# Softmax denominators inverted on one row per head and spread through device memory, normalisation by 512 columns, no clip, last products on the whole array

## The chip, the cores and the metric

The kernel runs on one NeuronCore of a Trainium2 chip. The metric is device time in microseconds of one execution (lower is better). The engines have these names in the profile: PE (matrix products), PEld (its weight loads), ACT (ScalarE), DVE (VectorE), POOL (GpSimd) and SP (SyncE, which here only issues transfers). Each takes its instructions strictly in the order in which the program lists them; an instruction that waits holds up all that are listed behind it on its engine. The order is fixed when the program is built.

## The reference

Two attention blocks read the same input, and a gate per token mixes them.

```python
def _A_ref(x, wq, wk, wv, wo):          # x: 1 x 2048 x 512, 32 heads of 16; one key and one value head
    q = (x @ wq).reshape(B, S, H, Dh).transpose(0, 2, 1, 3)
    k = x @ wk
    v = x @ wv
    p = _softmax(jnp.einsum("bhqd,bkd->bhqk", q, k) * (Dh ** -0.5), axis=-1)
    o = jnp.einsum("bhqk,bkd->bhqd", p, v)
    return o.transpose(0, 2, 1, 3).reshape(B, S, H * Dh) @ wo

def _B_ref(x, wqkv, wo):                # 32 heads with keys and values of their own
    ...

g = _sigmoid((x * gate_w).sum(-1, keepdims=True))
return g * a + (1 - g) * b              # a, b: the two blocks
```

All arrays are float32: x is 2048 by 512, the projections are 512 by 512 or narrower.

## The kernel before

**Groups and exps.** The 64 heads are worked in eight groups (`groups`: source "a" or "b", index 0 to 3) of eight heads. A group has two halves of 1024 queries; a half has four sums, numbered `s`, each for four pairs of a head and 512 queries over the 16 chunks `c` of 128 keys. A block is one head, one chunk and 512 queries. `scores(u)` makes two blocks with PE (keys on partitions, queries along the free dimension) in one of two PSUM tiles `sc`, and ACT takes their exp in one instruction of 128x1024 (line 569). There are 2048 such units, and some of them, listed in `vector`, don't go to ACT: `vector_scores` puts their products into a spare pair of PSUM banks, and DVE works out the exp by a polynomial in nine instructions: two of line 581, two of line 587 (`part`), five of line 592 (`horner`). `choose` decides while the program is built which units these are.

**Sums.** `values` multiplies the exps with the values and, in the same product, with ones, so that a sum has in each band of 32 rows 16 rows of the output and 16 equal rows of the denominator. Four banks `aux` form two pairs: one gathers the running sum, the other (`spare()`) is free for all other products, one at a time. After the last chunk `emptied` adds the two banks of the pair into `raw` with DVE (lines 229 and 230), and eight transfers from SP's queue take the denominators to a tile `dT` and the outputs to a tile `oT` (128 rows, 512 queries). When the second sum of a pair has come (`s % 2`), `norm_pieces` gives the side list eight tasks: four reciprocals of 128x128 (line 497), then four times a multiplication, a rounding to 16 bits and a remainder (lines 504 to 506). Each of the four adds one `o_unit`: three products of a 128-token tile with `wo` in 64x32 pieces of the PE array into two spare banks, then two additions to `acc` by DVE (line 485).

**Order.** `_Tasks` is a planner that runs while the program is built. It goes through the exps one after another (`EXP` = 916 ns each), keeps a clock for PE and a clock `busy` for DVE, and lists work when its numbers say that there is room: products from `units` (by due time), DVE tasks from `side` (each with an earliest step and a duration in ns; they are listed in the order of that step), polynomial pieces from `fill`. `late()` tells that products are behind and holds back new polynomial exps. `hurry` lists all side tasks that are due, before a sum is emptied. `flush` lists what is left after the last exp. The planner knows nothing of transfers: a side task of so many ns is reckoned to run at once.

**Other parts that the change touches.** `project` makes q and k from `x` (two additions, a clip by `QK_MAX`, line 394, then the split into two 16-bit parts). `flag_stats` collects the largest absolute values of inputs on DVE near the end (line 234); a flag from them selects a general path that isn't taken in these runs.

Below, a number of an exp counts ACT's instructions of line 569 (line 601 in the changed kernel) in the program's order from 0; a DVE or PE instruction "at exp 452" is one listed behind that exp and ahead of the next.

Of the kernel before, what the change touches and what calls it, by code (L numbers as in the profile page):

```python
# [12 lines left out]
F32 = mybir.dt.float32  # L13
# [7 lines left out]
P = 128  # L21
# [53 lines left out]
class _Tasks:  # L75
# [87 lines left out]
    def flush(self):  # L163

        assert not self.moves and not self.fill
        ahead = 0
        while self.open or self.units or self.side:
            if self.side and ahead < 6 and not (self.units and ahead > 2):
                self.side.popleft()[1]()
                ahead += 1  # L170
                continue
            ahead -= 3
# [15 lines left out]
def _fast(ctx, tc, x, wq_a, wk_a, wv_a, wo_a, wqkv_b, wo_b, gate_w, out, flag):  # L188
# [8 lines left out]
    ps_x = ctx.enter_context(tc.tile_pool(name="ps_x", bufs=1, space=PSUM))  # L197

# [127 lines left out]
    def kv_products(b, i, bank):  # L326
# [11 lines left out]
        k32 = ops.tile([P, 4, DH], F32, tag="k32", name=f"k32{b}")  # L338
# [25 lines left out]
    def project(w, needs, name, kind, n0, half, parts, put, queues, late=None):  # L364
# [16 lines left out]
        def product(i, c, a, b, first, last):  # L381
# [12 lines left out]
            nc.vector.tensor_scalar(y, y, QK_MAX, -QK_MAX, op0=ALU.min, op1=ALU.max)  # L394
# [72 lines left out]
    oT, dT, o16s = {}, {}, {}  # L467
# [23 lines left out]
    def norm_pieces(src, gi, half, t8, last):  # L491
        j, cols = t8 // 4, slice(t8 % 4 * P, (t8 % 4 + 1) * P)
        ends = last and half and j

        def over():
            d = dT[src, gi, half, j][:, cols]
            nc.vector.reciprocal(d, d)  # L497

        def parts():
            o, d = oT[src, gi, half, j][:, cols], dT[src, gi, half, j][:, cols]  # L500
            if t8 % 4 == 0:
                o16s[src, gi, half, j] = ops.tile([P, 2, BLK], F16, tag="o16", name=f"o16{src}{gi}{half}{j}", bufs=5)
            o16 = o16s[src, gi, half, j][:, :, cols]
            nc.vector.scalar_tensor_tensor(o, o, UP, d, op0=ALU.mult, op1=ALU.mult)
            (nc.scalar.copy if ends else nc.vector.tensor_copy)(o16[:, 0], o)  # L505
            (nc.gpsimd if ends else nc.vector).tensor_sub(o16[:, 1], o, o16[:, 0])
            todo.add([o_unit(src, gi, 8 * half + t8, o16, last)], todo.now + 4,
                     min(todo.now + 280, ends_by() - (0 if last and half else 60)))

        return [over, parts]  # L510
# [107 lines left out]
    def emptied(m):  # L618
        quad = blocks[4 * m : 4 * m + 4]
        n, half, s, c = quad[0][:4]  # L620
        src, gi = groups[n]
        todo.hurry()
        raw = ops.tile([P, BLK], F32, tag="raw", name=f"raw{src}{gi}{half}{s}", bufs=1)
        added(raw, aux[turn[0]], 1.0)
        j = quad[0][5]
        if s % 2 == 0:
            oT[src, gi, half, j] = ops.tile([P, BLK], F32, tag="oT", name=f"oT{src}{gi}{half}{j}", bufs=1)
            dT[src, gi, half, j] = ops.tile([P, BLK], F32, tag="dT", name=f"dT{src}{gi}{half}{j}", bufs=1)
        ends = m // NT == len(blocks) // 4 // NT - 1
        queues = (nc.sync, nc.scalar, nc.gpsimd) if ends else (nc.sync,)  # L630
        for a, part in enumerate((dT, oT)):
            for i, (_, _, _, _, p, _, hh) in enumerate(quad):
                rows = slice((2 * p + hh) * DH, (2 * p + hh + 1) * DH)

                at = 32 * i + (DH if (src == "a" or hh == 0) == (part is dT) else 0)
                queues[(4 * a + i) % len(queues)].dma_start(part[src, gi, half, j][rows], raw[at : at + DH, :])
        last = n == len(groups) - 1
        if s % 2:
            over, parts = zip(*[norm_pieces(src, gi, half, t8, last) for t8 in range(4 * j, 4 * j + 4)])
            todo.add_side(over, todo.now + (4 if last and half else 10), [950])  # L640
            todo.add_side(parts, todo.now + (4 if last and half else 13), [800])

    def flag_stats():
        absmax("v_a", 0, vA[:, :, :DH], AX.XY)
        for c in range(NK):
            absmax("x", c, xT[:, 0, c, :])
        absmax("gate", 0, wkv[:, :, 2 * DH])
        absmax("wk_a", 0, wkv[:, :, :DH], AX.XY)
        absmax("wv_a", 0, wkv[:, :, DH : 2 * DH], AX.XY)
# [23 lines left out]
    def begin(n, half):  # L673
# [291 lines left out]
```

## Time and profile before

| what | value |
|---|---|
| time, median of 3 runs | 1909.49 us (1907.66 to 1913.36) |
| the profiled execution: its own time | 1907.7 us |
| its span | 1905.9 us |
| mean granted PE clock | 0.992 |
| ACT busy | 1831.9 us |
| PE busy | 1800.7 us |
| DVE busy | 1382.3 us |
| first exp starts, last exp ends | 29.28 us, 1876.55 us |

The busy shares are of the whole span. PE's share counts pipelined matmuls whose ends are modelled, so 94% doesn't mean that PE has no room; the waits and the idle time ahead of an instruction tell which engine the others wait for.

### The profile page before, as it was taken

How to read it: one execution, taken by the hardware profiler on the slowest of the kernel's cores; microseconds unless marked ns; L12 is line 12 of the kernel's file. 1: busy time of each engine (PE TensorE's matmuls, PEld its weight loads, DVE VectorE, ACT ScalarE, POOL GpSimd, SP SyncE). 2: the span in 40 equal slices, each digit the busy share in tenths (PEclk: the TensorE clock that was granted, in tenths of full speed). 3: DMA queues.
4: the chain of work that ended last, by engine and by line, in shares of the span. 5: the costliest groups of instructions: out<-in, count | busy, mean ns of one | idle time of the engine just before them, and what ended most of it. 6: DMA issues, size and time to landing. Idle time of an engine off the chain costs nothing.

```text
span 1905.9 us, 128055 instructions
## 1 busy us (share of the span) xinstructions
PE 1800.7 (94%) x59664; PEld 1124.5 (59%) x59664; DVE 1382.3 (73%) x2095; ACT 1831.9 (96%) x1997; POOL 466.3 (24%) x840
## 2 busy tenths in 40 slices
PE   7999999999999999999999999999999999999985
PEld 4666665555566665665555656656655666665642
DVE  5367668787888765778788873788888867477762
ACT  4999999999999999999999999999999999999984
POOL 5333302330044230323006502042203433030000
PEclk9999999999999999999999999999999999999997
DMA  4121101110022110111002201020101111011101
GB/s 141 27 49 35 35 15 27 42 35 16 12 43 46 29 37 12 41 32 35 12 21 45 52 19 31 19 54 15 32 15 36 39 38 37 10 37 35 40 26 42
DMA packets 55739, 65.03 MB, mean 34 GB/s; under 512 B 21440, under 2 KB 29632, under 8 KB 55200
## 3 DMA queue, kind: packets, MB, share of 16 engines
q0 software_dynamic: 24112, 24.89, 6.8%
q1 hardware_dynamic: 30400, 31.46, 6.3%
q8 instruction: 469, 7.68, 1.7%
q14 instruction: 70, 0.57, 0.1%
q10 hardware_dynamic: 688, 0.43, 0.1%
HBM read 10.55 MB, written 4.19 MB: 8 GB/s over the span
## 4 chain that ended last, share of the span: by engine, by line
ACT 67%; PE 15%; issue 12%; DVE 4%; DMA 1%; SPq 0%; DVEq 0%; ACTq 0%; POOL 0%
ACT pr L569 67%; PE aux L613 7%; PE sc L562 4%; PE aux L225 4%; DVE stats L234 1%; DVE acc L485 0%; DVE vpr L592 0%; DMA acc<-in_A_x_dram 0%; DVE dTb L497 0%; DMA dTb<-rawb 0%; PE aux L300 0%; DVE v L238 0%; DVE yv L230 0%; DVE yv L229 0%; DVE xT L305 0%
## 5 line engine op out<-in xcount | busy, mean ns | idle before, releaser
L569 ACT ACTIVATE pr<-sc 128x1024 f32<-128x1024 f32 x1974 | 1821.3, 1090 | 24.7 <-PE sc L562 21.1
L613 PE MATMUL aux<-pr,vA 64*32 64x256 f32 x15712 | 647.2, 376 | 2.0 <-issue 1.8
L613 PE MATMUL aux<-pr,vB 64*32 64x256 f32 x15872 | 636.4, 376 | 0.6 <-issue 0.4
L562 PE MATMUL sc<-Qa,kA 64*32 64x512 f16 x7856 | 441.2, 380 | 28.0 <-ACT pr L569 4.7
L562 PE MATMUL sc<-Qb,K 64*32 64x512 f16 x7936 | 426.2, 381 | 31.0 <-ACT pr L569 5.6
L592 DVE SCALAR_TENSOR_TENSOR vpr<-vpr,part 128x1024 f32<-128x1024 f32 x296 | 363.5, 1228 | 6.1
L562 PEld LDWEIGHTS <-K 64*32 64x32 f16 x8192 | 203.3, 89 | 276.8 <-issue 195.3
L613 PEld LDWEIGHTS aux<-pr,vA 64*32 64x32 f32 x15712 | 328.6, 105 | 57.8 <-issue 9.8
L613 PEld LDWEIGHTS aux<-pr,vB 64*32 64x32 f32 x15872 | 316.6, 106 | 53.9 <-issue 4.6
L562 PEld LDWEIGHTS <-kA 64*32 64x32 f16 x8192 | 203.5, 89 | 238.8 <-issue 157.8
L485 DVE SCALAR_TENSOR_TENSOR acc<-aux,gate_up,acc 128x512 f32<-128x512 f32 x240 | 180.1, 750 | 126.6 <-PE aux L225 112.2
L375 POOL DMA_DIRECT2D Qb<-hib x128 | 63.0, 492 | 557.0 <-PE sc L562 553.9
L375 POOL DMA_DIRECT2D Qa<-hia x118 | 59.9, 508 | 481.8 <-PE sc L562 322.8
L581 DVE TENSOR_SCALAR vpr<-aux 128x512 int32<-128x512 f32 x148 | 95.2, 685 | 36.8 <-PE aux L562 36.2
L587 DVE TENSOR_SCALAR part<-vpr 128x1024 int32<-128x1024 int32 x148 | 103.1, 728 | 0.7
L375 POOL DMA_DIRECT2D K<-hik x128 | 64.3, 506 | 117.5 <-DVE hik L237 115.5
L592 DVE SCALAR_TENSOR_TENSOR vpr<-part 128x1024 f32<-128x1024 f32 x74 | 90.3, 1221 | 1.6
L225 PE MATMUL aux<-xT,w16vb 64*32 64x512 f16 x1536 | 90.5, 376 | 0.0
L225 PE MATMUL aux<-w16ob,o16b 64*32 64x512 f16 x1536 | 70.4, 391 | 16.0 <-ACT o16b L505 13.3
L225 PE MATMUL aux<-xT,w16kb 64*32 64x512 f16 x1536 | 79.5, 376 | 0.1
L225 PE MATMUL aux<-xT,w16qa 64*32 64x512 f16 x1536 | 76.0, 380 | 0.9 <-issue 0.5
L225 PE MATMUL aux<-xT,w16qb 64*32 64x512 f16 x1536 | 76.8, 376 | 0.0
(145 smaller groups left out, 1320.4 us busy)
## 6 DMA issues: line engine op xcount, KB each, us to landing
acc<-in_A_x_dram SPq DMA_DIRECT2D x16, 256.0 KB, 6.1
dTa<-rawa SPq DMA_DIRECT2D x128, 32.0 KB, 2.5
oTa<-rawa SPq DMA_DIRECT2D x128, 32.0 KB, 2.8
K<-hik POOLq DMA_DIRECT2D x128, 32.0 KB, 2.2
K<-lok POOLq DMA_DIRECT2D x128, 32.0 KB, 2.7
Qb<-hib POOLq DMA_DIRECT2D x128, 32.0 KB, 2.8
Qb<-lob POOLq DMA_DIRECT2D x128, 32.0 KB, 2.4
out_dram<-acc SPq DMA_DIRECT2D x16, 256.0 KB, 2.0
```

The costliest lines, as they stand in the source:

```text
L225: nc.tensor.matmul(out[n : n + COLS], lhsT[r, n : n + COLS], rhs[r], start=start, stop=stop)
L234: nc.vector.tensor_reduce(stats[:, n, i : i + 1], src, axis=axis, op=ALU.max, apply_absolute_value=True)
L375: queues[(8 * p + n) % len(queues)].dma_start(op[to : to + DH].rearrange("d (a q) -> d a q", a=2), state[part][rows])
L485: nc.vector.scalar_tensor_tensor(acc[:, t], bank, g, acc[:, t], op0=ALU.mult, op1=ALU.add)
L562: nc.tensor.matmul(sc[i][a : a + COLS], k[r, c * P + a : c * P + a + COLS], Q[src, gi, half, p][r, j * BLK : (j + 1) * BLK], start=True, s ...
L569: nc.scalar.activation(probs[u], sc, AF.Exp, scale=SCALE / (UP * UP))
L581: nc.vector.tensor_scalar(fix[:, i], sc[i], SCALE / (UP * UP) / math.log(2) * 2.0 ** 23, -(2.0 ** 23), op0=ALU.mult, op1=ALU.add)
L587: nc.vector.tensor_scalar(t, fix, a, b, op0=ALU.bitwise_and, op1=op)
L592: nc.vector.scalar_tensor_tensor(pr, pr if i < 4 else m, VEC[i], m if i else power, op0=ALU.add, op1=ALU.mult)
L613: nc.tensor.matmul(o[32 * i : 32 * i + 32, cols], v[r], probs[at // ACT][r, at % ACT, cols], start=first, stop=last)
```

## The change

- Where the denominators go: `emptied` no longer copies 16 equal rows per head to `dT`, but one row of 512 per head, folded to 16 partitions of 32 numbers, into a tile `few` of 128x32. `over` inverts that tile with one DVE instruction, writes it to device memory with one transfer (`bounce`), and reads it back with eight transfers, each of which repeats a row of 512 on 16 partitions of `dT`. All nine are on SP's queue. `few`, `dT` and `oT` have one buffer each.
- Normalisation: one multiplication, one rounding and one remainder over 128x512 (`divide`, `high`, `low`) in place of four of each over 128x128. The four `o_unit` are added together after `low`. The reciprocal may be listed 6 steps after the sum, `divide` 15 steps after it.
- The very last pair of sums keeps the old way of transfers, but each of four pieces runs through reciprocal, multiplication, rounding (ACT) and remainder (POOL), and `o_last` makes the last products with the whole array (three matmuls of 128x512 into one bank, one DVE addition), with stores on two queues.
- The clip of q and k in `project` is gone; `k32` has one buffer.
- `flag_stats` becomes eight tasks, from step 66 on in place of 60.
- `late()` allows 1.2 times as many products before it says late; `choose` allows up to 4 queued polynomial pieces (before 1) and 4000 ns of DVE backlog (before 1500).

```diff
-            if n > u[1] - self.now:
+            if n > (u[1] - self.now) * 1.2:
...
         while self.open or self.units or self.side:
-            if self.side and ahead < 6 and not (self.units and ahead > 2):
+            while self.side and not self.open:
                 self.side.popleft()[1]()
...
-            nc.vector.tensor_scalar(y, y, QK_MAX, -QK_MAX, op0=ALU.min, op1=ALU.max)
...
+    def o_last(src, gi, t, o16):
+        w, i = weights[src, gi, "o"], "ab".index(src)
+        bank = aux[t // 2 % 2][t % 2]
+        for n, (a, b) in enumerate(PARTS):
+            nc.tensor.matmul(bank, o16[:, a], w[:, b], start=n == 0, stop=n == 2)
+        nc.vector.scalar_tensor_tensor(acc[:, t], bank, gate_up[:, i, t : t + 1], acc[:, t], op0=ALU.mult, op1=ALU.add)
+        (nc.sync, nc.scalar)[t % 2].dma_start(out[t * P : (t + 1) * P, :], acc[:, t])
...
+        def over():
+            few = fews[key]
+            nc.vector.reciprocal(few, few)
+            bounce = dram.tile([8, DH, BLK // DH], F32, tag="few", name=f"few{src}{gi}{half}{j}")
+            nc.sync.dma_start(bounce.rearrange("h a b -> (h a) b"), few)
+            dT[key] = ops.tile([P, BLK], F32, tag="dT", name=f"dT{src}{gi}{half}{j}", bufs=1)
+            for h in range(8):
+                nc.sync.dma_start(dT[key][h * DH : (h + 1) * DH],
+                                  bounce[h : h + 1].rearrange("h a b -> h (a b)").broadcast_to([DH, BLK]))
+        def divide():
+            nc.vector.scalar_tensor_tensor(oT[key], oT[key], UP, dT[key], op0=ALU.mult, op1=ALU.mult)
+        def high():
...
+            nc.vector.tensor_copy(o16s[key][:, 0], oT[key])
+        def low():
+            nc.vector.tensor_sub(o16s[key][:, 1], oT[key], o16s[key][:, 0])
+            for t4 in range(4):
+                todo.add([o_unit(src, gi, 8 * half + 4 * j + t4, o16s[key][:, :, t4 * P : (t4 + 1) * P], last)],
+                         todo.now + 4, min(todo.now + 280, ends_by() - (0 if last and half else 60)))
+        todo.add_side([over], todo.now + 6, [300])
+        todo.add_side([divide, high, low], todo.now + 15, [700, 430, 700])
...
+                if a == 1 or ends:
+                    queue.dma_start((dT, oT)[a][key][rows], raw[at : at + DH, :])
+                else:
+                    queue.dma_start(fews[key][rows], raw[at : at + 1, :].rearrange("p (a b) -> p a b", a=DH))
...
-                todo.add_side([flag_stats], now + 60, [9000])
+                todo.add_side(flag_stats, now + 66, [2290] * NK + [420] * 4)
...
-        if asked or len(todo.fill) > 1 or todo.busy > todo.clock + 1500 or todo.late() or m < 3 * NT:
+        if asked or len(todo.fill) > 4 or todo.busy > todo.clock + 4000 or todo.late() or m < 3 * NT:
```

In the built program ACT has 1958 exps in place of 1974, and DVE works out 90 units in place of 74. Everything else on PE but the last four tiles is the same in number.

The first place is DVE's list where the pair of sums of group b0, second half, first 512 queries (`b010`) is normalised. Before:

```order
L485 SCALAR_TENSOR_TENSOR acc_90<-aux10_87,gate_up_100,acc_90 128x512
L485 SCALAR_TENSOR_TENSOR acc_90<-aux11_88,gate_up_100,acc_90 128x512
L497 RECIPROCAL dTb010_11638<-dTb010_11638 128x128 x4
L504 SCALAR_TENSOR_TENSOR oTb010_11637<-oTb010_11637,dTb010_11638 128x128
L505 CAST o16b010_12893<-oTb010_11637 128x128
L506 TENSOR_TENSOR o16b010_12893<-oTb010_11637,o16b010_12893 128x128
```

After (`vpr511` and `vpr510` are polynomial exps, `aux10` and `aux11` the spare banks at that time):

```order
L481 SCALAR_TENSOR_TENSOR acc_92<-aux10_89,gate_up_102,acc_92 128x512
L481 SCALAR_TENSOR_TENSOR acc_92<-aux11_90,gate_up_102,acc_92 128x512
L502 RECIPROCAL fewb010_11666<-fewb010_11666 128x32
L511 SCALAR_TENSOR_TENSOR oTb010_11665<-oTb010_11665,dTb010_12916 128x512
L515 CAST o16b010_12926<-oTb010_11665 128x512
L518 TENSOR_TENSOR o16b010_12926<-oTb010_11665,o16b010_12926 128x512
L613 TENSOR_SCALAR vpr511_12956<-aux10_89 128x512
L613 TENSOR_SCALAR vpr511_12956<-aux11_90 128x512
L624 SCALAR_TENSOR_TENSOR vpr510_12522<-vpr510_12522,part0510_12703 128x1024
L481 SCALAR_TENSOR_TENSOR acc_92<-aux10_89,gate_up_102,acc_92 128x512
```

The multiplication of line 511 now stands directly behind the reciprocal of line 502, and between the two lie, on SP's queue, the transfer to device memory and the eight back. Behind line 511 stand the two instructions that empty the spare banks (line 613).

The second place is SP's queue at the same pair of sums. Before:

```order
L636 DMA dTb010_11638<-rawb010_11634 16x512 x4
L636 DMA oTb010_11637<-rawb010_11634 16x512 x4
L636 DMA dTb010_11638<-rawb011_12392 16x512 x4
L636 DMA oTb010_11637<-rawb011_12392 16x512 x4
L636 DMA dTb011_13156<-rawb012_13152 16x512 x4
```

After:

```order
L676 DMA fewb010_11666<-rawb010_11662 16x1x32 x4
L674 DMA oTb010_11665<-rawb010_11662 16x512 x4
L676 DMA fewb010_11666<-rawb011_12445 16x1x32 x4
L674 DMA oTb010_11665<-rawb011_12445 16x512 x4
L504 DMA fewb010_12914<-fewb010_11666 128x32
L507 DMA dTb010_12916<-fewb010_12914 16x512 x8
L676 DMA fewb011_13205<-rawb012_13201 16x1x32 x4
```

Nine transfers are added for each pair of sums, and the eight reads stand behind the write that they need.

The third place is the end of DVE's list, the last sum (`rawb313`). Before:

```order
L230 SCALAR_TENSOR_TENSOR rawb313_53362<-aux11_88,rawb313_53362 128x512
L497 RECIPROCAL dTb311_52724<-dTb311_52724 128x128 x4
L504 SCALAR_TENSOR_TENSOR oTb311_52723<-oTb311_52723,dTb311_52724 128x128
L485 SCALAR_TENSOR_TENSOR acc_90<-aux00_85,gate_up_100,acc_90 128x512
L485 SCALAR_TENSOR_TENSOR acc_90<-aux01_86,gate_up_100,acc_90 128x512
L504 SCALAR_TENSOR_TENSOR oTb311_52723<-oTb311_52723,dTb311_52724 128x128
L485 SCALAR_TENSOR_TENSOR acc_90<-aux00_85,gate_up_100,acc_90 128x512
```

After (the pair of lines 536 and 537 comes four times):

```order
L227 SCALAR_TENSOR_TENSOR rawb313_53429<-aux11_90,rawb313_53429 128x512
L536 RECIPROCAL dTb311_52786<-dTb311_52786 128x128
L537 SCALAR_TENSOR_TENSOR oTb311_52785<-oTb311_52785,dTb311_52786 128x128
...
L493 SCALAR_TENSOR_TENSOR acc_92<-aux00_87,gate_up_102,acc_92 128x512
L493 SCALAR_TENSOR_TENSOR acc_92<-aux01_88,gate_up_102,acc_92 128x512
L493 SCALAR_TENSOR_TENSOR acc_92<-aux10_89,gate_up_102,acc_92 128x512
L493 SCALAR_TENSOR_TENSOR acc_92<-aux11_90,gate_up_102,acc_92 128x512
```

The eight additions that stood between the pieces have become four behind the last piece.

More of the change, by code (lines that the diff above doesn't have):

```diff
@@ new lines, in normalised_last, with piece @@
+    def normalised_last(src, gi, half, j):
+        key = (src, gi, half, j)
+        def piece(t4):
+            cols = slice(t4 * P, (t4 + 1) * P)
+            o, d = oT[key][:, cols], dT[key][:, cols]
+            if t4 == 0:
+                o16s[key] = ops.tile([P, 2, BLK], F16, tag="o16", name=f"o16{src}{gi}{half}{j}", bufs=5)
+            o16 = o16s[key][:, :, cols]
+            nc.vector.reciprocal(d, d)
+            nc.vector.scalar_tensor_tensor(o, o, UP, d, op0=ALU.mult, op1=ALU.mult)
+            nc.scalar.copy(o16[:, 0], o)
+            nc.gpsimd.tensor_sub(o16[:, 1], o, o16[:, 0])
+            todo.add([[lambda: o_last(src, gi, 8 * half + 4 * j + t4, o16)]], todo.now, todo.now)
+        todo.add_side([lambda t4=t4: piece(t4) for t4 in range(4)], todo.now + 4, [1800])
@@ L625, in emptied @@
         j = quad[0][5]
+        key = (src, gi, half, j)
+        ends = n == len(groups) - 1 and half and j
         if s % 2 == 0:
[L627 to L631, printed above, removed]
+            oT[key] = ops.tile([P, BLK], F32, tag="oT", name=f"oT{src}{gi}{half}{j}", bufs=1)
+            if ends:
+                dT[key] = ops.tile([P, BLK], F32, tag="dT", name=f"dT{src}{gi}{half}{j}", bufs=1)
+            else:
+                fews[key] = ops.tile([P, BLK // DH], F32, tag="few", name=f"few{src}{gi}{half}{j}", bufs=1)
@@ L632, in emptied @@
+        queues = (nc.sync, nc.scalar, nc.gpsimd) if ends and s % 2 else (nc.sync,)
+        for a in range(2):
             for i, (_, _, _, _, p, _, hh) in enumerate(quad):
                 rows = slice((2 * p + hh) * DH, (2 * p + hh + 1) * DH)
-                at = 32 * i + (DH if (src == "a" or hh == 0) == (part is dT) else 0)
-                queues[(4 * a + i) % len(queues)].dma_start(part[src, gi, half, j][rows], raw[at : at + DH, :])
-        last = n == len(groups) - 1
-        if s % 2:
-            over, parts = zip(*[norm_pieces(src, gi, half, t8, last) for t8 in range(4 * j, 4 * j + 4)])
-            todo.add_side(over, todo.now + (4 if last and half else 10), [950])
-            todo.add_side(parts, todo.now + (4 if last and half else 13), [800])
```

43 lines of the change are left out of this document (16 added, 27 removed).

## The prediction

> **What bounds the kernel now.** I read the page's busy times and chain first, then ACT's list in order of time, then the one stretch in which ACT stood still for long. First the page: span, busy times, the chain of work that ended last by engine, and the exp's group.
>
> ```profile
> span 1905.9 us, 128055 instructions
> PE 1800.7 (94%) x59664; PEld 1124.5 (59%) x59664; DVE 1382.3 (73%) x2095; ACT 1831.9 (96%) x1997; POOL 466.3 (24%) x840
> ACT 67%; PE 15%; issue 12%; DVE 4%; DMA 1%; SPq 0%; DVEq 0%; ACTq 0%; POOL 0%
> L569 ACT ACTIVATE pr<-sc 128x1024 f32<-128x1024 f32 x1974 | 1821.3, 1090 | 24.7 <-PE sc L562 21.1
> ```
>
> ACT's exps take 1821.3 of 1905.9 us and wait 24.7 in all. PE's 94% counts modelled ends, so the row for PE alone doesn't say who is the bound; ACT's timeline does:
>
> ```profile
> 1203.94 174.45 ACT L569 ACTIVATE pr<-sc 128x1024 f32<-128x1024 f32 x190 [0.46 <-PE sc L562]
> ```
>
> 190 exps follow each other without a gap, 174.45 / 190 = 0.918 us each: PE keeps up and ACT is the bound. So an exp that ACT doesn't do is worth 0.918 us, and a microsecond in which ACT stands still is lost for good. The only long stop of ACT between its first 30 exps and its last shows what stops it. Timeline of DVE, PE and ACT from 1812 to 1836 us (start, duration, instruction; in brackets the idle time before it and who ended it):
>
> ```profile
> 1812.28 8.86 DVE L234 TENSOR_REDUCE stats<-xT 128x1 f32<-128x2048 f16 x4
> 1827.93 1.77 DVE L497 RECIPROCAL dTb<-dTb 128x128 f32<-128x128 f32 x2 [5.08 <-DMA dTb<-rawb]
> 1829.61 1.51 DVE L485 SCALAR_TENSOR_TENSOR acc<-aux,gate_up,acc 128x512 f32<-128x512 f32 x2
> 1830.32 0.58 PE L225 MATMUL aux<-w16oa,o16a 64*32 64x512 f16 x1 [2.96 <-DVE acc L485]
> 1831.17 1.05 PE L225 MATMUL aux<-w16oa,o16a 64*32 64x512 f16 x15 [0.28 <-DVE acc L485]
> 1832.03 1.48 PE L613 MATMUL aux<-pr,vB 64*32 64x256 f32 x16
> 1835.56 0.63 PE L613 MATMUL aux<-pr,vB 64*32 64x256 f32 x16
> 1832.78 1.02 ACT L569 ACTIVATE pr<-sc 128x1024 f32<-128x1024 f32 x1 [4.48 <-PE sc L562]
> 1834.27 1.94 ACT L569 ACTIVATE pr<-sc 128x1024 f32<-128x1024 f32 x2 [0.47 <-PE sc L562]
> ```
>
> DVE waits 5.08 us for a transfer ahead of a reciprocal. Behind it stands the addition that empties the spare banks. PE needs these banks, waits 2.96 + 0.28 = 3.24 us with the next scores behind it, and ACT, which has only two score tiles, loses 4.48 + 0.47 = 4.95. The 1.7 us beyond PE's own wait are the restart: 16 value products take 1.48 us just after it and 0.63 again at 1835.56.
>
> The Trainium skill, "TensorE: Matmul & The Clock Gate", section "HAM oscillation — how this bites in real kernels", states that PE gaps over about 3.4 us bring the clock to half; half speed over one such window would lose 1.7 us by my estimate from its figure, and the row agrees, though its wait was 3.24.
>
> **The sum, part by part. Exps moved to DVE.** 16 fewer on ACT: 16 x 0.918 = 14.7 us saved. DVE pays, with these groups (busy, mean ns of one):
>
> ```profile
> L592 DVE SCALAR_TENSOR_TENSOR vpr<-vpr,part 128x1024 f32<-128x1024 f32 x296 | 363.5, 1228 | 6.1
> L587 DVE TENSOR_SCALAR part<-vpr 128x1024 int32<-128x1024 int32 x148 | 103.1, 728 | 0.7
> L581 DVE TENSOR_SCALAR vpr<-aux 128x512 int32<-128x512 f32 x148 | 95.2, 685 | 36.8 <-PE aux L562 36.2
> L497 DVE RECIPROCAL dTa<-dTa 128x128 f32<-128x128 f32 x64 | 55.7, 917 | 18.6 <-DMA dTa<-rawa 18.6
> L506 DVE TENSOR_TENSOR o16a<-oTa,o16a 128x128 f16<-128x128 f32 x64 | 18.7, 293 | 2.2
> L504 DVE SCALAR_TENSOR_TENSOR oTa<-oTa,dTa 128x128 f32<-128x128 f32 x64 | 17.5, 273 | 0.0
> L505 DVE CAST o16a<-oTa 128x128 f16<-128x128 f32 x64 | 14.6, 228 | 2.2
> L394 DVE TENSOR_SCALAR yk<-yk 128x512 f32<-128x512 f32 x16 | 6.8, 427 | 0.5
> L184 DVE RECIPROCAL gate_up<-z 128x16 f32<-128x16 f32 x1 | 0.3, 253 | 0.0
> L230 DVE SCALAR_TENSOR_TENSOR rawa<-aux,rawa 128x512 f32<-128x512 f32 x32 | 22.2, 692 | 3.4
> L237 DVE TENSOR_SCALAR v<-yv 128x512 f16<-128x512 f32 x16 | 6.9, 431 | 0.5
> ```
>
> A polynomial unit is 2 x 0.685 + 2 x 0.728 + 5 x 1.228 = 9.0 us, 16 of them 143. Taken away: 124 reciprocals, multiplications, roundings and remainders (124 x (0.917 + 0.273 + 0.228 + 0.293) = 212) and 48 clips (20). Added, 31 times: a 128x32 reciprocal, between 0.253 and 0.917, by width 0.35, then 0.69 + 0.43 + 0.69 by the 128x512 rows: 67. DVE does 22 us less than before, of 524 us that it has free: its load costs nothing. The clip, the counts and the planner's limits have no other price: what they move is in the 16 exps and in the places below.
>
> **The new round trip.** Reciprocal, write, eight reads, multiplication are a chain on SP's queue, and DVE waits at the multiplication. Rows by tile: issue on SP in ns (min/median/max), landing in us, for `dTb`, `out_dram`, `wob`, `wvb`:
>
> ```profile
> L636 SPq DMA_DIRECT2D dTb<-rawb x126: 507/589/1602, 303.3 to 1879.8; - x126
> DMA to landing us min/median/max: 1.9/2.2/4.0
> DMA to landing us min/median/max: 2.0/2.0/2.8
> DMA to landing us min/median/max: 2.9/3.1/3.9
> L261 SPq DMA_DIRECT2D wvb<-in_B_wqkv_dram x4: 380/448/453, 37.6 to 1281.6; - x4
> ```
>
> Reciprocal 0.35; write 2.0 (1.9 to 2.8, as the stores to device memory); the last of eight reads is issued 7 x 0.59 = 4.1 later (3.2 by the loads' 0.45, 4.5 with gaps); it lands 2.5 later, between 32 KB inside the chip (1.9) and 256 KB loads (2.9). Together 9.0 us, bounds 7.4 and 10.5. The Trainium skill, "DMA: Bandwidth & Descriptors", table "Specifications", says that pieces under 512 B are read, modified and written; `few` is written in pieces of 128 B, which no run here prices, and it would only lengthen the write.
>
> The planner leaves 9 steps (8.3 us) between reciprocal and multiplication, but only where the side list isn't held up. Where it is, both are listed back to back: so in 12 of 31 pairs, among them `b010` above, at exp 452. There DVE stands 9.0 us, then does W us of work until the banks are empty that PE needs D exps after the reciprocal. PE's wait is 9.0 + W - 0.916 D. At exp 452: W = 0.69 + 0.43 + 0.69 + 0.69 = 2.5, and PE's product with `w16ob0` into `aux10` comes at 457, D = 5: 9.0 + 2.5 - 4.6 = 6.9 us. In the same way at 205: D 6, W 2.4: 5.9; 330: 5, 2.5: 6.9; 392: 8, 5.0: 6.6; 512: 7, 2.5: 5.1; 572, 1060, 1548: 7, 2.6: 5.1 each; 632, 1120: 10, 3.2: 3.0 each; 1608: 10, 2.5: 2.3. At 1916 `hurry` puts the statistics ahead of the reciprocal (a polynomial piece of 1.2 us, two reductions of 8.86 / 4 = 2.2, four small ones, 0.8, begun about one exp early): DVE comes 5.5 us late, and PE needs the rounded tile at 1920: 5.5 + 9.0 + 1.1 - 3.7 = 12. Sum 67 us. It rests on DVE being on time where it meets the reciprocal, and this group of the page says so for before: DVE's additions wait for their products 92 times, 112 us, so that DVE is not behind.
>
> ```profile
> L485 DVE SCALAR_TENSOR_TENSOR acc<-aux,gate_up,acc 128x512 f32<-128x512 f32 x240 | 180.1, 750 | 126.6 <-PE aux L225 112.2
> ```
>
> The restart costs 1.7 each on the nine waits over 3.24: 15. In the other 19 pairs 8 to 22 exps lie between the two, the trip is nearly covered; I take 0 (10 at the upper bound). Together 82; by the bounds of the trip 47 (no restart counted) to 116.
>
> **Statistics.** The stop of 4.95 us at 1828 goes with the task of 9 us; what is late next is the place at 1916, counted. Saved 4.95.
>
> **The end.** Timeline of DVE and POOL from 1877 us:
>
> ```profile
> 1877.71 0.69 DVE L229 TENSOR_SCALAR rawb<-aux 128x512 f32<-128x512 f32 x1 [19.31 <-PE aux L613]
> 1882.50 3.39 DVE L497 RECIPROCAL dTb<-dTb 128x128 f32<-128x128 f32 x4 [3.29 <-DMA dTb<-rawb]
> 1887.52 0.42 POOL L506 TENSOR_TENSOR o16b<-oTb,o16b 128x128 f16<-128x128 f32 x1 [6.80 <-issue]
> 1888.68 1.62 DVE L485 SCALAR_TENSOR_TENSOR acc<-aux,gate_up,acc 128x512 f32<-128x512 f32 x2 [2.65 <-PE aux L225]
> 1899.36 1.61 DVE L485 SCALAR_TENSOR_TENSOR acc<-aux,gate_up,acc 128x512 f32<-128x512 f32 x2 [1.59 <-PE aux L225]
> ```
>
> Four pieces of 0.85 + 0.27 from 1882.50 end at 1887.0, four additions of 0.75 follow, and POOL (0.42 a piece) and PE run beside: 1890.0 in place of 1900.97. Saved 10.9 (8 if a piece of PE work ends late).
>
> **Sum.** 82 - 14.7 - 4.95 - 10.9 = +51 on the profiled execution's 1907.7 us (span 1905.9): 1959. The median shown is 1.8 above that execution: 1961.
>
> **Rivals.** *The trip is covered.* If DVE ran ahead of the plan by some five exps, or the trip took under about 5.5 us, the waits would add up to less than the 30.6 us saved; with none, 1909.5 - 30.6 = 1879, faster. For it: DVE's four waits for `dTa` (18.6 us in the group of line 497) stopped ACT nowhere for long, since PE needed nothing behind them. Against it: the trip's rows give nothing under 7.4, and at the twelve places a bank is needed 4 to 10 exps later. *PE becomes the bound.* With the 14.7 us not won: 1976. Against it: the 190 exps without a gap. *DVE falls behind and stays so.* The trip at its upper bound, the queue of polynomial pieces (now up to 4) late behind it: 116 - 30.6 on 1909.5 gives 1995; for it speaks that both values and banks wait for DVE's list.
>
> **How the numbers follow.** The waits as computed: 0.66 (1935 to 1985). DVE behind for good: 0.12. PE as the bound, besides: 0.05. Covered: 0.13. Something near no change, the trip by half shorter: 0.04. Forecast 1961, range 1925 (lower bound of the trip, no restart: 1909.5 - 30.6 + 47) to 2000 (upper bound). Within 0.3% is about what a measurement here can't tell from no change: faster 0.13, same 0.04, slower 0.83.
>
> **What would show it.** DVE rows of line 511 idle for 7 to 10 us "<-DMA" in about 12 places; ACT waits of 3 to 8 us there, with a sum of idle time before line 601 near 100 us (24.7 - 4.95 + 82); 1958 exps; the last addition 13 to 14 us after the last exp (before 24.4). Line 511 with waits under 3 us would prove me wrong, and so would long waits there with PE's scores on time.

## The result and the profile after

| | time before | time after | ratio (95% interval) |
|---|---|---|---|
| median | 1909.77 us (1906.07 to 1913.36) | 2003.42 us (1999.26 to 2009.73) | 1.0494 (1.0470 to 1.0517) |

The changed kernel is slower by 94 us, where 51 were forecast, and above the range's upper end. The profiled execution's span grew from 1905.9 to 1997.5 us, and the mean granted PE clock fell from 0.992 to 0.97. The page of after: span, busy times, the chain of work that ended last by engine, and the exp's group (busy, mean ns of one, idle time ahead).

```profile
span 1997.5 us, 127898 instructions
PE 1819.8 (91%) x59580; PEld 1140.0 (57%) x59580; DVE 1366.3 (68%) x1815; ACT 1824.6 (91%) x1981; POOL 465.8 (23%) x840
ACT 46%; PE 22%; issue 11%; DVE 9%; DMA 6%; SPq 6%; DVEq 0%; ACTq 0%; POOLq 0%; POOL 0%
L601 ACT ACTIVATE pr<-sc 128x1024 f32<-128x1024 f32 x1958 | 1813.6, 1078 | 132.2 <-PE sc L594 126.9
```

In the chain ACT's share fell from 67% to 46%. DMA rose from 1 to 6% and SP's queue from 0 to 6%: the new round trip now stands in the chain. ACT's idle time ahead of its exps is 132.2 us in place of 24.7. Nearly all of the loss is in that one number. The waits of DVE and PE (us in total, times, longest) say what is behind it:

```profile
DVE oTa L511 <- DMA dTa<-fewa: 75.4, 13, 8.9
DVE oTb L511 <- DMA dTb<-fewb: 51.3, 11, 8.6
DVE v L234 <- PE aux L450: 8.9, 3, 3.1
PE aux L222 <- DVE acc L481: 23.8, 12, 6.1
PE aux L222 <- DVE vpr L613: 18.4, 3, 6.7
PE aux L645 <- DVE vB L457: 7.8, 3, 2.9
```

DVE waits 127 us at line 511, and PE waits for the DVE work listed behind it. One such place in order of time, the pair `b010` at exp 452 that the prediction worked through (start, duration, instruction; in brackets the idle time before it and who ended it):

```profile
484.36 0.34 DVE L502 RECIPROCAL fewb<-fewb 128x32 f32<-128x32 f32 x1
484.73 0.35 SPq L504 DMA_DIRECT2D fewb<-fewb  x1
486.19 4.25 SPq L507 DMA_DIRECT2D dTb<-fewb  x8
492.11 0.69 DVE L511 SCALAR_TENSOR_TENSOR oTb<-oTb,dTb 128x512 f32<-128x512 f32 x1 [7.40 <-DMA dTb<-fewb]
493.90 1.28 DVE L613 TENSOR_SCALAR vpr<-aux 128x512 int32<-128x512 f32 x2
494.64 1.65 PE L222 MATMUL aux<-w16ob,o16b 64*32 64x512 f16 x16 [5.90 <-DVE vpr L613]
496.85 1.02 ACT L601 ACTIVATE pr<-sc 128x1024 f32<-128x1024 f32 x1 [7.17 <-PE sc L594]
```

The reciprocal starts at 484.36. The write is issued at 484.73, the first read can be issued at 486.19, the eight issues last 4.25 us, and the multiplication starts at 492.11, 7.75 us after the reciprocal. DVE does the rounding, the remainder and the first step of a polynomial unit; only then is PE's bank empty. PE stood 5.90 us, ACT 7.17 (and 0.68 after its first exp).

What the stop does to PE's clock is seen in the same place (stretch; length, busy us of PE, PEld, DVE, ACT, POOL; granted clock, DMA share, GB/s):

```profile
486.00:489.00 3.00, 2.52 (x72) 1.24 (x72) 0.00 (x0) 3.00 (x5) 0.00 (x0) 1.00 0.13 38
492.00:494.50 2.50, 0.00 (x0) 0.00 (x0) 2.33 (x4) 0.00 (x0) 0.00 (x0) 0.58 0.00 0
495.50:497.00 1.50, 1.50 (x40) 0.75 (x32) 0.82 (x1) 0.15 (x1) 0.00 (x0) 0.50 0.00 0
499.00:502.00 3.00, 2.79 (x95) 1.62 (x87) 2.97 (x4) 2.90 (x4) 0.00 (x0) 0.96 0.00 0
801.00:802.00 1.00, 0.69 (x26) 0.48 (x33) 1.00 (x6) 0.00 (x0) 0.00 (x0) 1.00 0.00 0
```

After PE's idle 5.90 us the clock is at 0.50 until about 499; after the shorter wait of 2.88 us that ended at 801.30 it stayed at 1.00. The Trainium skill, "TensorE: Matmul & The Clock Gate", section "Part 1: The HAM clock gate (the "warmup" mystery)", states that one idle window of about 3.4 us halves the clock and one busy window brings it back. Both places agree with it. A third is less clear: in the kernel before, PE's waits of 2.96 and 0.28 us near 1830 us, with a single product between them, were followed by a clock of 0.59 (1830 to 1832) and 0.56 (1832 to 1834). So 3.4 us is no sharp bound for one wait.

ACT's stops in the trace, put together by where they stand:

| where | forecast | measured |
|---|---|---|
| the 12 back-to-back places | 82 | 86.8 |
| pairs whose reciprocal directly follows its sum (exps 256, 682, 811, 1170, 1299, 1658, 1787) | 0 | 13.8 |
| three places at the v units (exps 744, 1232, 1720) | not in the sum | 9.3 |
| all others (before: 19.75, and the stop of 4.95) | 19.75 | 22 |
| ACT idle, difference to before | +77 | +107.5 |
| 16 exps fewer | -14.7 | -7.7 |
| last exp's end to the end of the program | -10.9 | -7.7 |
| first exp's start | 0 | -0.9 |
| span | +51 | +91.6 |

The second row's place at exp 811 shows why 8 steps and more didn't cover the trip there:

```profile
849.63 3.33 SPq L674 DMA_DIRECT2D oTb<-rawb  x4
853.41 0.34 DVE L502 RECIPROCAL fewb<-fewb 128x32 f32<-128x32 f32 x1
853.78 0.34 SPq L504 DMA_DIRECT2D fewb<-fewb  x1
856.53 4.68 SPq L507 DMA_DIRECT2D dTb<-fewb  x8
864.28 0.69 DVE L511 SCALAR_TENSOR_TENSOR oTb<-oTb,dTb 128x512 f32<-128x512 f32 x1 [3.55 <-DMA dTb<-fewb]
869.26 1.02 ACT L601 ACTIVATE pr<-sc 128x1024 f32<-128x1024 f32 x1 [2.72 <-PE sc L594]
```

Four transfers of the same sum, 32 KB each, had been issued just ahead. The first read could only be issued 2.75 us after the write (1.46 at exp 452), the eight issues took 4.68 us (4.25), the multiplication started 3.07 us after their end (1.67), and the trip took 10.87 us; in such pairs it took 10.7 to 13.6. What stands ahead in the queue isn't the whole cause of a late write: at exp 330 SP had issued nothing for 8 us, and the first read still came 3.28 us after the write (355.07 to 358.35).

The third row is another mechanism. The change's planner limits list the fourth v unit's product ahead of the transposes of the third (the expectations below call them third and second, or second and first). At exp 744:

```profile
798.25 0.43 DVE L234 TENSOR_SCALAR v<-yv 128x512 f16<-128x512 f32 x1 [3.11 <-PE aux L450]
801.30 0.83 PE L645 MATMUL aux<-pr,vB 64*32 64x256 f32 x13 [2.88 <-DVE vB L457]
802.50 2.86 ACT L601 ACTIVATE pr<-sc 128x1024 f32<-128x1024 f32 x3 [2.80 <-PE sc L594]
```

`v16` has one buffer, so its next split (line 234) waits for the transposes; and value products wait for `vB`, which comes out of these. On DVE the copy into `vB` (line 457, at 800.97) stands behind that split and behind a multiplication of line 511 (800.36).

### The profile page after: what moved, and what is told of

Same layout as the page of the kernel before. It is cut to its first block, busy times and chain, and to the rows that moved or that the text cites. A ratio compares the mean times of both kernels' runs of the same rounds, so it can differ in the third digit from the quotient of the medians.

```text
span 1997.5 us, 127898 instructions
## 1 busy us (share of the span) xinstructions
PE 1819.8 (91%) x59580; PEld 1140.0 (57%) x59580; DVE 1366.3 (68%) x1815; ACT 1824.6 (91%) x1981; POOL 465.8 (23%) x840
## 4 chain that ended last, share of the span: by engine, by line
ACT 46%; PE 22%; issue 11%; DVE 9%; DMA 6%; SPq 6%; DVEq 0%; ACTq 0%; POOLq 0%; POOL 0%
ACT pr L601 46%; PE aux L645 10%; PE sc L594 6%; PE aux L222 4%; SPq L507 4%; DMA dTa<-fewa 2%; DVE vpr L624 1%; DMA fewa<-fewa 1%; DMA dTb<-fewb 1%; DMA fewb<-fewb 1%; DVE stats L231 1%; SPq L676 1%; SPq L674 1%; DVE acc L481 1%; DMA fewb<-rawb 1%
## 5 line engine op out<-in xcount | busy, mean ns | idle before, releaser
L601 ACT ACTIVATE pr<-sc 128x1024 f32<-128x1024 f32 x1958 | 1813.6, 1078 | 132.2 <-PE sc L594 126.9
L594 PE MATMUL sc<-Qb,K 64*32 64x512 f16 x7824 | 439.3, 385 | 35.9 <-ACT pr L601 14.6
L594 PE MATMUL sc<-Qa,kA 64*32 64x512 f16 x7840 | 447.8, 386 | 22.8 <-ACT pr L601 3.9
L624 DVE SCALAR_TENSOR_TENSOR vpr<-vpr,part 128x1024 f32<-128x1024 f32 x360 | 445.4, 1237 | 7.7
L645 PEld LDWEIGHTS aux<-pr,vB 64*32 64x32 f32 x15648 | 323.8, 107 | 72.3 <-issue 10.9
L481 DVE SCALAR_TENSOR_TENSOR acc<-aux,gate_up,acc 128x512 f32<-128x512 f32 x232 | 174.0, 750 | 98.0 <-PE aux L222 83.7
L613 DVE TENSOR_SCALAR vpr<-aux 128x512 int32<-128x512 f32 x180 | 115.5, 683 | 23.0 <-PE aux L594 22.4
L619 DVE TENSOR_SCALAR part<-vpr 128x1024 int32<-128x1024 int32 x180 | 121.6, 703 | 0.5
L624 DVE SCALAR_TENSOR_TENSOR vpr<-part 128x1024 f32<-128x1024 f32 x90 | 110.9, 1232 | 2.3
L222 PE MATMUL aux<-w16oa,o16a 64*32 64x512 f16 x1536 | 80.3, 388 | 18.7 <-DVE vpr L613 6.7
L222 PE MATMUL aux<-xT,w16vb 64*32 64x512 f16 x1536 | 80.7, 376 | 0.0
```

Of the source, the lines that this page charges most:

```text
L222: nc.tensor.matmul(out[n : n + COLS], lhsT[r, n : n + COLS], rhs[r], start=start, stop=stop)
L481: nc.vector.scalar_tensor_tensor(acc[:, t], bank, g, acc[:, t], op0=ALU.mult, op1=ALU.add)
L594: nc.tensor.matmul(sc[i][a : a + COLS], k[r, c * P + a : c * P + a + COLS], Q[src, gi, half, p][r, j * BLK : (j + 1) * BLK], start=True, s ...
L601: nc.scalar.activation(probs[u], sc, AF.Exp, scale=SCALE / (UP * UP))
L613: nc.vector.tensor_scalar(fix[:, i], sc[i], SCALE / (UP * UP) / math.log(2) * 2.0 ** 23, -(2.0 ** 23), op0=ALU.mult, op1=ALU.add)
L619: nc.vector.tensor_scalar(t, fix, a, b, op0=ALU.bitwise_and, op1=op)
```

## The experiments

Theory: DVE's wait at line 511 for the round trip makes the loss, where the program lists reciprocal and multiplication close together (101 us with the pairs behind a sum), and three places at the v units make 9 more. Rival 1: the looser planner limits overload DVE with polynomial pieces, and the wait only takes a share of that. Rival 2: PE, at a lower clock, has become the bound. The time before drifted (medians 1909.8, 1916.0, 1920.7, 1915.4 in the four sets of runs), so each ratio is to the time before of the same set; "scaled" below is a ratio times 1909.8.

**The wait taken away.** Line 511 alone is edited; it multiplies by a constant tile, so the division by the denominators is left out.

```diff
-            nc.vector.scalar_tensor_tensor(oT[key], oT[key], UP, dT[key], op0=ALU.mult, op1=ALU.mult)
+            nc.vector.scalar_tensor_tensor(oT[key], oT[key], UP, vA.rearrange("p a b -> p (a b)"), op0=ALU.mult, op1=ALU.mult)
```

> The changed kernel with every instruction and transfer kept; only the multiplication of line 511 reads a constant tile (the values of branch a, 128x512) in place of dT, so the division by the denominators is left out and DVE waits for no round trip. Theory (DVE waits for the round trip at line 511, in 12 back-to-back places and, shorter, in 7 places where the reciprocal follows its sum): the 87 + 14 us of ACT's stops there go, 2003 - 101 = 1902 us, 1893 to 1912; the idle time ahead of line 601 falls from 132 to 25 to 40 us. Rival 1 (the looser planner limits: DVE's longer queue of polynomial pieces makes values and banks late, and the wait only takes a share of that): at most a third goes, 1965 or more. Rival 2 (PE with its lower clock has become the bound, 1819.8 us busy against 1800.7): 1980 or more.

1902.72 us, ratio 0.9921 (0.9898 to 0.9943). Its clock is 0.991. The exp's group on its page:

```profile
L601 ACT ACTIVATE pr<-sc 128x1024 f32<-128x1024 f32 x1958 | 1812.5, 1078 | 39.4 <-PE sc L594 34.1
```

With all instructions and transfers in place, 93 of the 132 us of idle time went with the one dependency, and the time was below that of before. Both rivals' numbers (1965, 1980 or more) are missed by 60 us and more. What remains holds the v units' stops (2.87, 2.89 and 2.39 us).

**One read in place of eight.**

```diff
-            for h in range(8):
-                nc.sync.dma_start(dT[key][h * DH : (h + 1) * DH],
-                                  bounce[h : h + 1].rearrange("h a b -> h (a b)").broadcast_to([DH, BLK]))
+            nc.sync.dma_start(dT[key], bass.AP(tensor=bounce.tensor, offset=bounce.offset,
+                                               ap=[[BLK, 8], [0, DH], [1, BLK]]))
```

> The changed kernel with one read of the whole bounced tile, spread 16 times by its access pattern, in place of eight reads; same order, same 1958 exps. Theory: seven issues of about 0.5 us leave the trip, which falls from 8.4 to about 5 us; 12 x 3.4 = 41 us and most of the 14 us of the seven places go, and the clock comes back in some places: 1950 us, 1940 to 1962. Rival 1 (planner limits) and rival 2 (PE the bound): within 10 us of 2003. Rival 3 (landing, not issuing, makes the trip: a read of all 128 partitions takes as long as eight): trip at 7 us or more, 1985 or more.

1957.54 us, ratio 1.0208 (1.0185 to 1.0231); clock 0.981. The same pair `b010`, and the exp's group:

```profile
475.40 0.34 DVE L502 RECIPROCAL fewb<-fewb 128x32 f32<-128x32 f32 x1
475.77 0.35 SPq L504 DMA_DIRECT2D fewb<-fewb  x1
477.24 0.65 SPq L506 DMA_DIRECT2D dTb<-fewb  x1
481.23 0.69 DVE L510 SCALAR_TENSOR_TENSOR oTb<-oTb,dTb 128x512 f32<-128x512 f32 x1 [5.49 <-DMA dTb<-fewb]
L600 ACT ACTIVATE pr<-sc 128x1024 f32<-128x1024 f32 x1958 | 1813.1, 1079 | 92.3 <-PE sc L593 87.2
```

The trip is 5.83 us here in place of 7.75; over the 12 places 6.1 on average in place of 8.3. ACT's idle time falls by 40 us. The time follows the length of the trip, as the theory says, but the trip didn't get down to the expected 5: the issues fell from 4.25 to 0.65 us, while the multiplication started 3.34 us after the end of the one issue, against 1.67 after the end of eight. So the third rival of this run, the landing, had a share. The Trainium skill, "DMA: Bandwidth & Descriptors", section "Anatomy of one DMA — SWDGE (gpsimd) path", gives a transfer a fixed cost of about 2 us, most of it the receipt from the target memory, by a fit for POOL's queue. In the changed kernel, on SP's queue, the first read could be issued 1.46 us after the write at this pair and 2.75 us at exp 811; no run here splits a landing into its parts.

**The multiplication moved away from the reciprocal.** It is put on the list when the reciprocal is really listed.

```diff
         def over():
...
+            todo.add_side([divide, high, low], todo.now + 15, [700, 430, 700])
...
         todo.add_side([over], todo.now + 6, [300])
-        todo.add_side([divide, high, low], todo.now + 15, [700, 430, 700])
```

> The changed kernel with the multiplication listed at least 15 steps after the step at which the reciprocal is really listed, in place of 15 steps after the sum: 13.8 us between the two in every pair, eight reads as before, 1960 exps. Theory: the trip of 8.4 us (12 at most) is covered in all pairs, line 511 waits under 10 us in all, and ACT's 87 + 14 us go: 1904 us, 1893 to 1915. Rival 1 (planner limits): the late values stay, 1965 or more. Rival 2 (PE the bound): 1980 or more.

1901.05 us, ratio 0.9919 (0.9899 to 0.9939). In thirteen pairs this order puts the multiplication behind the next pair's first transfers into `oT`, so it multiplies other rows than it should; its time stands for the schedule. The second version bounds it:

```diff
         if s % 2 == 0:
+            while pend:
+                pend.popleft()()
             oT[key] = ops.tile([P, BLK], F32, tag="oT", name=f"oT{src}{gi}{half}{j}", bufs=1)
```

(`pend` holds the three steps of a pair; the side tasks take them from it.)

> The changed kernel with the multiplication listed at least 15 steps after the step at which the reciprocal is really listed, but no later than the next pair's first sum, so that the rows of oT are read before new ones land in them. Eight reads, limits and end as in the changed kernel; 1960 exps; the distance between reciprocal and multiplication is 12 steps (11.0 us) at least. Theory: as in the run with 15 steps and no such bound, 0.992 of the time before: 1892 to 1906 where before takes 1911 to 1916. If the bound hands DVE its work at a bad moment (together with the sum), up to 10 us more.

1906.26 us, ratio 0.9935 (0.9915 to 0.9956), clock 0.994. The waits at the multiplication (line 514 there) and the exp's group:

```profile
DVE oTa L514 <- DMA dTa<-fewa: 7.3, 3, 3.6
DVE oTb L514 <- DMA dTb<-fewb: 0.3, 1, 0.3
L603 ACT ACTIVATE pr<-sc 128x1024 f32<-128x1024 f32 x1960 | 1811.6, 1077 | 38.5 <-PE sc L596 24.1
```

The same round trip with eight reads, the same limits and the same end cost 127 us of waits in after and 7.6 here; the time is that of the run without the dependency, within the two intervals. The cost was the place of the multiplication, not the trip as such.

**The limits alone, and the change without them.**

```diff
-            if n > u[1] - self.now:
+            if n > (u[1] - self.now) * 1.2:
...
-        if asked or len(todo.fill) > 1 or todo.busy > todo.clock + 1500 or todo.late() or m < 3 * NT:
+        if asked or len(todo.fill) > 4 or todo.busy > todo.clock + 4000 or todo.late() or m < 3 * NT:
```

On the kernel before:

> The kernel before with the changed kernel's two planner limits (late by 1.2; four pieces and 4000 ns in choose) and nothing else; 1970 exps on ACT, four fewer than before. Theory: 4 x 0.918 = 3.7 us less, and the 9 us of the three places where the new order puts a v unit's product ahead of the transposes of the unit before it: +5 us, ratio 1.000 to 1.005. Rival 1 (the limits make DVE late and are the cause of the changed kernel's loss): 30 us or more above before, ratio 1.015 or more.

1936.68 us, ratio 1.0083 (1.0062 to 1.0103): 16 us, between the two theories' numbers. ACT's timeline near 650 us and at the v units, and its exp's group:

```profile
649.86 1.94 ACT L569 ACTIVATE pr<-sc 128x1024 f32<-128x1024 f32 x2 [1.69 <-PE aux L613]
654.25 1.94 ACT L569 ACTIVATE pr<-sc 128x1024 f32<-128x1024 f32 x2 [2.44 <-PE aux L613]
755.49 1.02 ACT L569 ACTIVATE pr<-sc 128x1024 f32<-128x1024 f32 x1 [3.15 <-PE sc L562]
L569 ACT ACTIVATE pr<-sc 128x1024 f32<-128x1024 f32 x1970 | 1821.3, 1083 | 46.4 <-PE sc L562 34.1
```

The three places at the v units make about 10 us, as expected. Besides, ACT waits for value products (near 361 and 650, 8.8 us in all): the looser order lists these so late that the tile that an exp writes isn't free. That was not in the theory. So the limits have a price of their own, and four exps didn't pay for it.

On the changed kernel the old limits put back:

> The changed kernel with the two planner limits of before; 1966 exps. In this order only 8 pairs have reciprocal and multiplication within 4 steps, the others lie 7 to 14 steps apart. Theory (the round trip of 8.4 us against the steps to the first use, 11 us where the reciprocal follows its sum directly): 42 us of waits and 12 us of restarts in place of 101, the 9 us of the v units go, 8 exps come back (7 us): 2003 - 56 + 7 = 1954, 1940 to 1970. Rival 1 (the limits are the cause by DVE's load): 1915 or less. Rival 2 (PE's bound): 1985 or more. If the limits had nothing to do with where reciprocal and multiplication meet: 2001.

1974.15 us, ratio 1.0259 (1.0229 to 1.0288), scaled 1959, against 1954 expected. Two of its stops, at pairs that are still back to back (exps 516 and 698), and the group:

```profile
542.89 1.02 ACT L601 ACTIVATE pr<-sc 128x1024 f32<-128x1024 f32 x1 [6.66 <-PE sc L594]
718.53 1.02 ACT L601 ACTIVATE pr<-sc 128x1024 f32<-128x1024 f32 x1 [6.84 <-PE sc L594]
L601 ACT ACTIVATE pr<-sc 128x1024 f32<-128x1024 f32 x1966 | 1822.1, 1075 | 103.8 <-PE sc L594 100.4
```

The limits alone cost 16 us, all other parts together 49, and the two together 94. One stop at a v unit stays with the old limits (3.28 us). About 29 us belong to neither edit alone (21 to 37 by the three intervals). They fit the pairs in which the two edits meet. With the old limits nothing stands on DVE between reciprocal and multiplication in 8 pairs, and two instructions in a ninth; ACT stops for about 59 us at these nine. With the new limits it is 11 pairs and one instruction in a twelfth, and about 87 us. No run isolates this share.

**Two buffers for `v16`** (`bufs=2` for `v16`, 4 in place of 5 for `o16` to make room).

> The changed kernel with two buffers for v16 (four in place of five for o16 make the room); same order. Theory for the three places where the second v unit's split waits for the first's transposes (line 234 on line 450, 8.9 us in 3): ACT's 9 us there go, 1994 us, 1990 to 1999. Rival: these stops come from the order of PE's work and not from the buffer: 2001 or more. If four o16 tiles are too few, new waits ahead of the rounding show, and the time rises.

2010.05 us, ratio 1.0483 (1.0458 to 1.0507): no difference that shows against after's 1.0494. Line 234 no longer waits, but ACT's stops at the v units are 0.84, 3.77 and 2.14 us, in after 2.80, 2.39 and 2.75. Exp 1232 shows why:

```profile
1278.13 0.69 DVE L511 SCALAR_TENSOR_TENSOR oTa<-oTa,dTa 128x512 f32<-128x512 f32 x1 [3.80 <-DMA dTa<-fewa]
1278.74 0.88 DVE L457 TENSOR_SCALAR vB<-aux 128x128 f32<-128x128 f32 x4
1279.08 1.29 PE L645 MATMUL aux<-pr,vB 64*32 64x256 f32 x16 [3.19 <-DVE vB L457]
1280.92 1.02 ACT L601 ACTIVATE pr<-sc 128x1024 f32<-128x1024 f32 x1 [3.77 <-PE sc L594]
```

Now the multiplication ahead of the copy into `vB` waits for the round trip: 1.75, 3.80 and 2.44 us at the three places, in after 0.35, 0.03 and 0. In after the two waits lie one over the other, so taking one away leaves the other, and this run doesn't tell the buffer from the order. In the run without the dependency only line 234 waits there (9.0 us in 3), and ACT stops for 2.4 to 2.9 us: there the buffer and the late transposes are enough. Two buffers without the wait for the trip were not tried.

**The end alone**, on the kernel before (`o_last`, `normalised_last` and the new `flush`).

> The kernel before with only the changed kernel's end: the last four pieces as reciprocal, multiplication, rounding and remainder in one go, their products on the whole array (512 columns, three matmuls each) with one addition and one store each; 1974 exps as before. Theory: the time between the last exp's end and the end of the program falls from 29.4 to 21.6 us: 7.7 us less, ratio 0.995 to 0.997. By the prediction 10.9 us, 0.994. Rival (the end depends on the stores and not on the pieces): no change.

1910.26 us, ratio 0.9943 (0.9923 to 0.9963): 10.9 us, and the interval holds 7.7 too. Its timeline gives the smaller number. The last exps, and the last two additions:

```profile
1847.58 42.46 ACT L593 ACTIVATE pr<-sc 128x1024 f32<-128x1024 f32 x46 [0.68 <-PE sc L586]
1904.98 0.75 DVE L493 SCALAR_TENSOR_TENSOR acc<-aux,gate_up,acc 128x512 f32<-128x512 f32 x1 [0.53 <-PE aux L492]
1906.26 0.75 DVE L493 SCALAR_TENSOR_TENSOR acc<-aux,gate_up,acc 128x512 f32<-128x512 f32 x1 [0.53 <-PE aux L492]
```

The last exp ends at 1890.04, the last addition at 1907.01, 17.0 us later (before 24.4). The interval of the ratio reaches from about 7 to 15 us, so the two numbers don't contradict each other.

**What is best of it.** Three versions of the bounded retimed kernel with one read (with the late limit of before, with `choose`'s, with both), and the kernel before with only the new end and the statistics in eight tasks.

> The retimed kernel (multiplication 15 steps after the reciprocal, at the latest at the next first sum) with one read in place of eight and the late limit of before; choose keeps the new limits; 1962 exps. In this order each v unit's transposes stand ahead of the next unit's product in all 16 places. Theory: no wait for the trip, no stop at the v units (about 9 us of the retimed kernel's), two exps more (1.8 us): 0.989 of the time before, 0.986 to 0.991. Rival: the stops near the v units come from the longer queue of polynomial pieces that choose lets in: 0.993 as the retimed kernel.

1895.84 us, ratio 0.9889 (0.9867 to 0.9912): as expected, and the fastest version of all. No wait at the multiplication, none of line 234 and none for `vB` is left in its trace.

> The same with the two limits the other way round: choose's limits of before, late by 1.2; 1968 exps. In this order the second v unit's transposes come behind the third unit's product, as in the changed kernel, in three places. Theory: these places cost their 9 us again and eight exps more cost 7 us: 0.997, 0.995 to 1.000. Rival (the pieces that choose lets in make the stops): stops gone, 0.991.

1903.13 us, ratio 0.9934 (0.9915 to 0.9952): less slow than expected. Line 234's wait is back, as the order said, but it costs ACT 1.69, 1.83 and 1.66 us (0.77 + 0.89), 5.2 and not 9:

```profile
DVE v L234 <- PE aux L450: 9.1, 3, 3.1
749.80 2.86 ACT L602 ACTIVATE pr<-sc 128x1024 f32<-128x1024 f32 x3 [1.69 <-PE sc L595]
```

So the same order costs 9 us in after and about 5 here. At the first of the three places the traces show the difference on DVE, between the wait of line 234 and the copy into `vB`. Here only the rest of the split and a statistics task stand there, and PE waits 1.84 us for `vB`. In after the multiplication of line 511 stands there too, with 0.35 us of its own wait, and PE waits 2.88; in the run with the limits alone it is a reciprocal of 0.94 us, and PE waits 2.63. Neither side of that expectation was right.

> The same with both limits of before; 1970 exps, ten more than the retimed kernel (9.2 us). The v units' transposes come behind the next product in two of the three places (6 us): 0.996, 0.993 to 0.999. What is left between this and before is the end, the split statistics and four exps less what the v units cost, so nothing of the trip.

1900.21 us, ratio 0.9928 (0.9908 to 0.9948), at the fast edge of the expected band: the v units' order, in two places, again costs less than 3 us each (1.69 us at the larger).

> The kernel before with the changed kernel's end and its statistics in eight tasks; division as before, 1972 exps. Theory: the end's 10.9 us (0.994 measured alone), the 5 us stop at 1828 us and two exps (1.8 us): 0.991, 0.988 to 0.993. If the statistics only move the stop: 0.994.

1902.59 us, ratio 0.9932 (0.9913 to 0.9951). Of the statistics' stop 2.28 us are left in ACT's list. The interval holds the upper end of the expected band and the rival's 0.994, so the time doesn't tell them apart. The fastest version, with the round trip, is 0.4% below this one by the medians, and their intervals just miss each other (0.9912, 0.9913). So a small gain is likely; which part of that version brings it wasn't tried (it has 1962 exps, this one 1972).

## Why the prediction was right and wrong

**Direction and mechanism: right.** DVE waits at line 511 for the trip, in the 12 places named, behind it PE and then ACT; the runs without the dependency and with the multiplication moved show that this wait is the loss.

**The 12 places, 82 us: 86.8 measured.** The trip was a little shorter (8.3 us on average against 9.0, 8 us over the 12), the restart a little longer (at exp 452 ACT stood 7.85 us in all for PE's 5.90: 1.95 against 1.7), and the three places for which I counted none lost more than forecast (at exp 1608 about 4.1 us against 2.3). So a part of the fit is luck: errors that cancel.

**"In the other 19 pairs ... I take 0": wrong.** This is the first step that failed. I took one trip for all pairs. Where the reciprocal follows its sum, the write goes out behind the sum's own four transfers, the trip is 10.7 to 13.6 us instead of 9.0, and ACT lost 13.8 us. Of the 3.1 us between exp 811 and exp 452, 1.3 are in the write, 0.4 in the issues and 1.4 in the landing of the reads. My own upper bound for this step was 10.

**"The clip, the counts and the planner's limits have no other price": wrong.** The limits alone cost 16 us, the v units' share of it 9.3 in after. I had looked in the order at the pairs only, not at the v units.

**16 exps, -14.7: -7.7 in the trace.** 0.918 us is the pace of exps without a gap. An exp behind a stop takes 1.02, as the rows at 496.85 and 869.26 show, and there are 92 waits in place of 36. Exps saved are worth less in a kernel in which ACT stops more often.

**The end, -10.9: -7.7 in the trace.** I let four additions follow each other in 0.75 us each. Two of them come 1.28 us after the one ahead, since they wait 0.53 us for the three products on the whole array, and the first started 12.4 us after the last exp's end, 2.0 later than reckoned. The last addition ended 16.5 us after the last exp, not 13 to 14.

**The statistics:** as forecast, the stop at 1828 went and the next one, 10.45 us at exp 1916, came in its place (12 forecast).

The errors add up to +4.8 + 13.8 + 9.3 + 2.2 + 7.0 + 3.2 - 0.9 = 39 of the 41 us between +51 and +91.6, all but one to the same side. Of the rivals none took place, though the time is nearest to that of "DVE falls behind and stays so" (1995): DVE's load fell to 1366.3 us, and its additions still waited 84 times, 83.7 us, for PE's products, so that DVE was not behind. PE's lower clock goes with the stops (0.97 in after, 0.991 to 0.994 in the runs without the long waits).

What stays open is why the same write is done after 1.4 us in most back-to-back pairs and after 3.3 us at exp 330, and whether the 29 us that the limits and the other parts cost only together lie in the pairs alone.

## What to carry to other kernels

Put a consumer's place in a list at a distance from where its producer is really listed, not from the event that should have listed both: here the same round trip cost 100 us or nothing. Price a transfer chain for each place, by what its queue has just issued ahead of it and with its spread (7.1 to 13.6 us here), and a stop of the bounding engine by more than its length: the clock behind it and the overlap that is broken count too. Two edits that each move a list have to be priced together, since what they cost only together (about 29 of 94 us here) belongs to neither. One wait on an engine can hide a second one behind it: taking the first away then gains nothing, as with the two buffers.

## What was not expected of the hardware

- One read of the whole tile, spread 16 times by its access pattern, was issued in 0.65 us where eight took 4.25, but the multiplication started 3.34 us after the end of that issue, against 1.67: of 3.6 us saved in issuing, 1.7 were given back in landing.
- The same 16 KB write was done 1.46 us after its issue at exp 452, where nothing stood just ahead of it, and 2.75 us at exp 811, behind four transfers of 32 KB inside the chip; but also 3.28 us at exp 330, with nothing issued for 8 us.
- PE's clock was at 0.50 for about 4.5 us of work behind a wait of 5.90 us and not reduced at all behind one of 2.88; in the kernel before, waits of 2.96 and 0.28 us with one product between them were followed by 0.59 and 0.56.
